# Feed-forward row pairs in one group of 12, masks summed early, last down products by output halves

## The chip, the cores and the metric

The kernel runs on one core of a Trainium2 chip. The metric is the device time of one execution in microseconds (us). Engines are named as in the profile: PE (TensorE) multiplies, PEld is its weight load, DVE is VectorE, ACT is ScalarE, POOL is GpSimd, SP only issues transfers here. PE writes its products to PSUM, eight banks of 512 float32 numbers per partition, and DVE and ACT read them from there.

## The reference

A row of 2048 tokens of 448 numbers goes through four layers: attention A, feed-forward B, A, B, with the same weights in both rounds.

```python
x = x + _A_ref(_layernorm(x), mem0, Wq, Wk, Wv, Wo, 32)
x = x + _B_ref(_layernorm(x), W_gate, W_up, W_down)
x = x + _A_ref(...)   # again, and B again
```

A runs over 64 segments of 32 tokens. Each segment is put behind a memory of 8 rows; 16 heads attend over these 40 rows (memory rows see all, token rows only earlier tokens); the first 8 rows of the output are the memory of the next segment. So the segments are a recurrence. B is, per token, `(relu(x Wg) * (x Wu)) Wd` with 1792 hidden numbers.

## The kernel before

Before the loop the kernel folds the weights: Wq with Wk into `A_sb`, Wv with Wo into `B_sb`, so that a step of the recurrence is: project the 40 rows by `A_sb` (PSUM tiles `prj`), scores of memory rows (`Sm`) and of token rows (`Sx`), softmax, weighting (`y`, `ya`, `yb`), projection by `B_sb` (`ox`, `o3`). The heads are taken in two halves, `hf` 0 and 1.

Both rounds run at once: chain 0 is the first A, chain 1 the second, four segments (LAG) behind. `step(g, ...)` (L679) does segment g of chain 0 and g-4 of chain 1. With two chains (g = 4 to 63) a step's matmuls have 80 columns, with one chain 40. Every second step, odd g from 3, also has a feed-forward: a `Feed` (L466) of 64 tokens of the first B and 64 of the second, 128 columns. The last two feeds have only 64. Steps run to g = 68; a tail behind them (L991 to L1008) finishes the last two feeds.

The order of work is written out by hand. `mm` (L142) chains all matmuls in the order in which the code issues them, and `InOrder` (L92) does so for DVE and ACT. So each engine is a queue in the order of the source, and an instruction that waits holds up all behind it on its engine. PSUM banks are given out by `bank` (L120): it takes the bank that, by a running estimate of PE's time (`now`) and a time `after` for each kind of tile, comes free first; `hold=True` keeps it until `let_go` (L130). A matmul into a bank waits for the last reader of the tile that was there.

A feed has 14 tiles of 128 hidden numbers, in groups u = 0 to 3 of 4, 4, 4 and 2. 448 input rows are three chunks of 128 and one of 64. The 64-row rest of Wu stands in partitions 0 to 63 of chunk 3, that of Wg in 64 to 127 (`FR`), and `xT` holds the rest of the tokens in both. `open_rows` (L493) issues these rests as row pairs: two matmuls of 64 rows each, one for `ups`, one for `gps`, which run side by side. It takes held banks, two a group. `products(u)` (L510) adds the three full chunks, 12 matmuls each for ups and gps, and lets the banks go. `gated(u)` (L521) copies ups to `ut` on ACT and writes `hh = max(gps, 0) * ut` on DVE. `down_part` (L530) multiplies `hh` by `Wd_sb` into `dps`, and `down_out` (L548) adds the residual and sends rows out.

`softmax` (L641) returns three closures: `first` (with two chains the mask is added into the SBUF tile `se`; then maximum and subtraction), `exp` on ACT, `second` (sum, reciprocal, and the product into `PM` or `PX`). m1, x0 and x1 are those of Sm and Sx of a half. `flipped` (L668) transposes PM or PX on PE (tile `pps`) and copies the result (`PT`). `weigh_m` (L749) makes ya and yb from PT and `hk`. `project_out(hf, t0, t1)` (L796) issues three ox matmuls for each of the tiles t0 to t1 of 28. `feed_on` (L572) turns the rows for the step after next into `hT` (through `tps`).

The part of a step with a feed around the change is L920 to L947, behind both `scores`: rows of groups 0 and 1, softmax x0, groups 0 and 1, flip of PM1, rows of groups 2 and 3, flip of PX0, group 2, weigh_m, group 3, all of softmax x1, 8 tiles of project_out, down, the rest. The last step with a feed (`end`, g = 67) is L904 to L919.

With one chain, the mask is a matmul of `ident` by `maskS` into Sx. With m and x both asked for, `scores` (L709) does the key chunks 0, 1, 3 of Sm, the mask, those of Sx, and then chunk 2 of both.

In the last two feeds `down_part` puts even tiles of hh in output partitions 0 to 63 and odd ones in 64 to 127, as column pairs side by side; `down_out` then copies the upper half by ACT (`other`), and DVE adds both to `x`.

Of the kernel before, what the change touches and what calls it, by code (L numbers as in the profile page):

```python
# [8 lines left out]
BF = mybir.dt.bfloat16  # L9
F32 = mybir.dt.float32  # L10
# [34 lines left out]

KD = (0, 1, 3, 2)
FR = (slice(0, 64), slice(64, 128))


def upper(hf, t):  # L50
# [9 lines left out]
def build_kernel(ctx, tc, A_x, A_mem0, A_Wq, A_Wk, A_Wv, A_Wo, B_W_gate, B_W_up, B_W_down, out,  # L60
# [69 lines left out]
    def let_go(t):  # L130

        i, after = bank_of[t.name]
        held.discard(i)
        free_at[i] = now[0] + after
# [80 lines left out]
    def weights(dst, src):  # L215
        return [(dst[:, k, cols], src[128 * k:128 * k + 128, cols])
                for k in range(3) for cols in (slice(0, F // 2), slice(F // 2, F))] + [
                    (dst[FR[src is B_W_gate], 3, :], src[384:448])]

    pieces = weights(Wu_sb, B_W_up)  # L220

    def next_piece():
# [235 lines left out]
    nc.gpsimd.memset(hh[:], 0.0)  # L458

    Wg_sb = main.tile([P, 4, F], BF, name="Wg_sb")  # L460
    pieces += weights(Wg_sb, B_W_gate)
    Wd_sb = main.tile([P, FT, DM], BF, name="Wd_sb")
    for f in range(FT):
# [2 lines left out]
    class Feed:  # L466
# [10 lines left out]
        def residual(self):  # L477
            tp = bank([P, 4, 128], BF, "otp")
            for kd in range(4):
                tr(tp[:, kd, :], OT[:, kd, :], ident[:])  # L480
            dve.tensor_tensor(self.x[:], tp[:].rearrange("p k d -> p (k d)")[:, 0:DM], self.x[:], op=ALU.add)
            self.st = row_stats(self.x)

        def norm(self):
            self.xn = normed(self.st)
# [7 lines left out]
        def open_rows(self, us):  # L493

            n = self.n
            self.ps = getattr(self, "ps", {})
            for u in us:
                self.ps[u] = [bank([P, 4, 128], F32, name, after, hold=True) for name, after in (("ups", 1000), ("gps", 1600))]
            for u in us:
                for e in range(min(4, FT - 4 * u)):  # L500
                    f = 4 * u + e
                    for W_sb, ps, rows in zip((Wu_sb, Wg_sb), self.ps[u], FR):
                        mm(ps[:, e, n], W_sb[rows, 3, f * 128:(f + 1) * 128], xT[rows, 3, n],
                           start=(e == 0), stop=False, skip_group_check=True)
# [5 lines left out]
        def products(self, u):  # L510
            n = self.n
            k = min(4, FT - 4 * u)
            for W_sb, ps in zip((Wu_sb, Wg_sb), self.ps[u]):
                for e in range(k):
                    f = 4 * u + e
                    for kd in range(3):
                        mm(ps[:, e, n], W_sb[:, kd, f * 128:(f + 1) * 128], xT[:, kd, n],
                           start=False, stop=(kd == 2), skip_group_check=True)
                let_go(ps)

        def gated(self, u):  # L521
            n = self.n
# [7 lines left out]
        def down_part(self, f0, f1):  # L530
            if f0 == 0:
                self.dps = bank([P, 512], F32, "dps", hold=True)
            dps = self.dps
            for f in range(f0, f1):
                if self.first:
                    mm(dps[:, 0:DM], hh[:, f, :], Wd_sb[:, f, :], start=(f == 0), stop=(f == FT - 1))
                else:
                    r = slice(64 * (f % 2), 64 * (f % 2) + 64)
                    mm(dps[r, 0:DM], hh[:, f, 0:TB], Wd_sb[:, f, :], start=(f < 2), stop=(f >= FT - 2),
                       tile_position=(0, r.start), skip_group_check=True)  # L540
            if f1 == FT:
                let_go(dps)

# [4 lines left out]
        def down_out(self):  # L548
            i, dps = self.i, self.dps
            if self.first:  # L550
                dve.tensor_tensor(self.nx[TB:P, :], dps[TB:P, 0:DM], self.x[TB:P, :], op=ALU.add)
                self.st = row_stats(self.nx)
                nc.sync.dma_start(xa[(i + 2) % 3][0:TB, :], self.nx[TB:P, :])
            if self.second and not self.first:
                other = main.tile([P, DM], F32, tag="other", name="other")
                act.copy(other[0:TB, :], dps[TB:P, 0:DM])
                dve.tensor_tensor(self.x[0:TB, :], dps[0:TB, 0:DM], self.x[0:TB, :], op=ALU.add)
                dve.tensor_tensor(self.x[0:TB, :], other[0:TB, :], self.x[0:TB, :], op=ALU.add)
                nc.sync.dma_start(out_dram[block(i - LAG // BLK)], self.x[0:TB, :])
            elif self.second:  # L560
                dve.tensor_tensor(self.x[0:TB, :], dps[0:TB, 0:DM], self.x[0:TB, :], op=ALU.add)
                nc.sync.dma_start(out_dram[block(i - LAG // BLK)], self.x[0:TB, :])
            if self.first and i + 3 < nblk:
                nc.sync.dma_start(self.x[TB:P, :], x_dram[block(i + 3)])
# [76 lines left out]
    def softmax(Sp, n, dst, keep, tag, mask=None):  # L641

        mx = main.tile([P, n], F32, tag=f"mx{tag}", name="mx")
        se = main.tile([P, n, L], F32, tag=f"se{tag}", name="se")
        ssum = main.tile([P, n], F32, tag=f"ssum{tag}", name="ssum")
        rs = main.tile([P, n], F32, tag=f"rs{tag}", name="rs")

        def first():
            src = Sp
            if mask is not None:  # L650
                dve.tensor_tensor(se[:], Sp[:], mask, op=ALU.add)
                src = se
            dve.tensor_reduce(mx[:], src[:], axis=AX.X, op=ALU.max)
            dve.tensor_tensor(se[:], src[:], mx[:].unsqueeze(2).to_broadcast([P, n, L]), op=ALU.subtract)

        def exp():
            act.activation(se[:], se[:], AF.Exp, scale=SCALE)

        def second():
            dve.tensor_reduce(ssum[:], se[:], axis=AX.X, op=ALU.add)  # L660
            dve.reciprocal(rs[:], ssum[:])
            if keep is not None:
                dve.tensor_tensor(rs[:], rs[:], keep, op=ALU.mult)
            dve.tensor_tensor(dst[:, :, 0:L], se[:], rs[:].unsqueeze(2).to_broadcast([P, n, L]), op=ALU.mult)

        return first, exp, second

    def flipped(src, n, tag, eng=dve):  # L668
        pps = bank([P, n, 128], BF, "pps")
# [9 lines left out]
    def step(g, ff, pre, late):  # L679
# [29 lines left out]
        def scores(hf, m, x):  # L709
# [21 lines left out]
                if not both:  # L731
                    mm(Sx[:, :, :], ident[:], maskS[:], start=True, stop=False, skip_group_check=True)

            if m and x:
                mem(KD[:3])
                mask()
                own(KD[:3])
                mem(KD[3:])
                own(KD[3:])
            elif m:  # L740
                mem(KD)
            elif x:
                mask()
                own(KD)
            sm = softmax(Sm, 2, PM[hf], blk[:], f"m{hf}") if m else (lambda: None,) * 3
            sx = softmax(Sx, 4, PX[hf], None, f"x{hf}", maskS[:] if both else None) if x else None
            return sm, sx

# [122 lines left out]
        def memory_0():  # L871
            nonlocal m0
            m0, _ = scores(0, True, False)
            m0[0]()
            m0[1]()

        if late is not None:
# [20 lines left out]
        _, x0 = scores(0, False, True)  # L898
        weigh_m(0, hk, pm)
        m1, x1 = scores(1, True, True)  # L900
        m1[0]()
        m1[1]()
        x0[0]()
        if end:  # L904
            ff.open_rows((0, 1))
            x0[1]()
            x1[0]()
            x1[1]()
            x0[2]()
            ff.products(0)  # L910
            ff.products(1)
            px0 = flipped(PX[0], 2, "x0", act)
            x1[2]()
            ff.gated(0)
            ff.gated(1)
            weigh_x(0, hk, px0)
            px1 = flipped(PX[1], 2, "x1", act)
            weigh_x(1, hk, px1)
            return {}, None  # L919
        if ff is not None:  # L920
            ff.open_rows((0, 1))
            x0[1]()
            m1[2]()
            x0[2]()
            feed(0, 1)
            next_piece()
            pm = flipped(PM[1], 1, "m1", act) if ms else None
            ff.open_rows((2, 3))
            px0 = flipped(PX[0], 2, "x0", act)
            feed(2)  # L930
            weigh_m(1, hk, pm)
            feed(3)
            x1[0]()
            x1[1]()
            x1[2]()
            ox_open()
            project_out(0, 0, 8)
            next_piece()
            ff.down()
            ff.norm2()  # L940
            project_out(0, 8, NT)
            project_last()
            next_piece()
            project_out(1, 0, 12)
            px1 = flipped(PX[1], 2, "x1")
            ff.feed_on()
            project_out(1, 12, NT)  # L947
        else:
            next_piece()
            ox_open()  # L950
            x0[1]()
            m1[2]()
            late_flip = 23
# [1 line left out]
            pm = flipped(PM[1], 1, "m1") if ms else None  # L955
            project_out(0, late_flip, NT)
            weigh_m(1, hk, pm)
            x1[0]()
            x1[1]()
            x0[2]()  # L960
# [28 lines left out]
            pre, late = step(g, None, pre, late)  # L989

    ff = Feed(nblk + LAG // BLK - 1)  # L991
    fed.open_rows((2, 3))
    ff.residual()
    for u in (2, 3):
        fed.products(u)
# [5 lines left out]
    ff.xposed()  # L1001
    ff.xposed_out()
    fed.down_out()
    for us in ((0, 1), (2, 3)):
        ff.open_rows(us)
        for u in us:
            ff.gate_up(u)
    ff.down()  # L1008


# [56 lines left out]
```

## Time and profile before

| what | value |
| --- | --- |
| median of 3 runs | 1585.41 us (1585.05 to 1586.82) |
| the profiled execution | 1585.9 us |
| its span | 1583.8 us |
| PE busy | 1570.4 us (99%) |
| DVE busy | 1130.9 us (71%) |
| ACT busy | 753.1 us (48%) |
| POOL busy | 77.4 us (5%) |
| mean granted PE clock | 0.998 |

The span runs from the first to the last instruction of the trace. "Busy" of PE is modelled, since matmuls overlap; a matmul's cost in a stream is the distance of its start to the next start, not its duration. A timeline line gives start, duration, engine, line of the code, operation, tiles (written <- read), shapes, how many were merged into it, and in brackets how long the engine had been idle and what ended that. L101, L143 and L151 are the helpers through which most instructions are recorded, so tiles tell them apart. The chain of waits is followed back from the last instruction to what released each.

### The profile page before, as it was taken

Reading aid. Unit: us, or ns where it says so; the run is one execution under the profiler, and the core shown is the slowest. Engines: PE = TensorE matmul, PEld = TensorE weight load, DVE = VectorE, ACT = ScalarE, POOL = GpSimd, SP = SyncE. Lnnn points to the kernel's source line nnn. Section 1 sums busy time; section 2 is a strip of 40 time slices with the busy share of each in tenths; the row PEclk is TensorE's granted clock in tenths of the full one; section 3 lists DMA queues with packets and bytes.
Section 4 is the critical chain, followed back from the end, with each engine's and each line's share of the span. In section 5 each row is a group of like instructions: output and inputs, shape, how many; then the busy total and the mean of one; then the engine's idle time right before and its main releaser. Section 6 shows DMA issues by size and latency. Waiting matters only on the chain.

```text
span 1583.8 us, 89753 instructions
## 1 busy us (share of the span) xinstructions
PE 1570.4 (99%) x41132; PEld 1444.0 (91%) x41132; DVE 1130.9 (71%) x3706; ACT 753.1 (48%) x2090; POOL 77.4 (5%) x172
## 2 busy tenths in 40 slices
PE   9999999999999999999999999999999999999998
PEld 6698999999999999999999999999999999999897
DVE  8766777777677777776777777767777777677764
ACT  5754444454444444544444445444444454444443
POOL 3200000000000000000000000000000000000000
PEclk9999999999999999999999999999999999999999
DMA  8620000000000000000000000000000000000000
GB/s 245 202 78 9 8 10 9 8 5 10 9 10 9 10 10 9 4 10 10 9 10 9 9 9 4 10 10 9 10 9 10 9 4 10 9 8 6 7 7 6
DMA packets 27755, 33.12 MB, mean 21 GB/s; under 512 B 3560, under 2 KB 26480, under 8 KB 27376
## 3 DMA queue, kind: packets, MB, share of 16 engines
q1 hardware_dynamic: 26288, 23.70, 5.4%
q8 instruction: 321, 5.26, 1.4%
q0 software_dynamic: 1088, 3.68, 0.8%
q14 instruction: 58, 0.48, 0.1%
HBM read 23.70 MB, written 1.84 MB: 16 GB/s over the span
## 4 chain that ended last, share of the span: by engine, by line
PE 97%; DVE 1%; ACT 0%; DMA 0%; issue 0%; SPq 0%; POOLq 0%; POOL 0%; ACTq 0%
PE prj L143 31%; PE ox L143 25%; PE ups L143 7%; PE dps L143 5%; PE gps L143 5%; PE o L143 5%; PE y L143 4%; PE Sx L143 3%; PE pps L151 2%; PE bps L143 1%; PE aps L143 1%; PE Sm L143 1%; PE tpw L151 1%; PE ya L143 1%; PE kps L151 1%; PE tps L151 1%
## 5 line engine op out<-in xcount | busy, mean ns | idle before, releaser
L143 PE MATMUL prj<-hT,A_sb 128*128 128x80 bf16 (+3 forms) x15232 | 541.6, 199 | 0.1
L143 PEld LDWEIGHTS <-A_sb 128*128 128x128 bf16 (+1 forms) x15232 | 498.5, 99 | 23.0 <-issue 0.6
L143 PEld LDWEIGHTS <-B_sb 128*128 128x128 bf16 (+1 forms) x15232 | 492.7, 103 | 13.7 <-issue 0.2
L143 PE MATMUL ox<-Y,B_sb 128*128 128x80 bf16 (+3 forms) x11424 | 441.7, 200 | 0.1
L101 ACT CAST TQ<-prj 128x480 bf16<-128x480 f32 (+1 forms) x380 | 184.2, 497 | 102.9 <-PE prj L143 96.2
L101 ACT CAST Y<-y 128x512 bf16<-128x512 f32 (+2 forms) x392 | 137.2, 419 | 94.8 <-PE y L143 94.6
L101 DVE CAST Y<-y 128x256 bf16<-128x256 f32 x376 | 151.4, 457 | 42.2 <-PE y L143 42.0
L101 ACT ACTIVATE se<-se 128x80 f32<-128x80 f32 (+1 forms) x270 | 81.9, 303 | 181.3 <-DVE se L101 177.0
L143 PE MATMUL gps<-xT,Wg_sb 128*128 128x128 bf16 (+3 forms) x1904 | 137.2, 215 | 0.0
L143 PE MATMUL ups<-xT,Wu_sb 128*128 128x128 bf16 (+3 forms) x1904 | 134.7, 216 | 0.5 <-DVE xT L101 0.5
L101 DVE CAST TQ<-prj 128x480 bf16<-128x480 f32 (+1 forms) x228 | 128.6, 573 | 6.8 <-PE prj L143 6.4
L143 PEld LDWEIGHTS <-Wu_sb 128*128 128x128 bf16 (+1 forms) x1904 | 106.1, 97 | 10.3
L143 PEld LDWEIGHTS <-hk 40*128 40x128 bf16 (+1 forms) x1950 | 99.7, 96 | 14.1 <-issue 3.0
L101 DVE SCALAR_TENSOR_TENSOR hh<-gps,ut 128x512 bf16<-128x512 f32 (+2 forms) x136 | 77.6, 591 | 45.0 <-PE ya L143 40.7
L143 PEld LDWEIGHTS <-Wg_sb 128*128 128x128 bf16 (+1 forms) x1904 | 108.0, 97 | 0.5 <-issue 0.5
L101 ACT CAST TZ<-prj 64x320 bf16<-64x320 f32 (+2 forms) x264 | 96.9, 378 | 17.2 <-DVE TZ L101 13.6
L101 ACT COPY os<-o 64x16 f32<-64x16 f32 (+3 forms) x135 | 25.7, 191 | 163.2 <-PE o L143 161.6
L101 DVE TENSOR_REDUCE ssum<-se 128x2 f32<-128x80 f32 (+1 forms) x270 | 73.8, 273 | 37.1 <-ACT se L101 37.1
L143 PE MATMUL y<-PT,hk 40*128 40x256 bf16 (+1 forms) x1280 | 91.2, 248 | 1.9 <-ACT PT L101 1.0
L143 PE MATMUL dps<-Wd_sb,hh 128*128 128x448 bf16 (+1 forms) x476 | 93.1, 353 | 0.0
L143 PEld LDWEIGHTS <-TQ 128*128 128x128 bf16 x1938 | 86.7, 97 | 1.6 <-issue 1.3
L101 ACT COPY PT<-pps 128x256 bf16<-128x256 bf16 (+1 forms) x136 | 47.2, 347 | 81.1 <-PE pps L151 76.9
(118 smaller groups left out, 1881.1 us busy)
## 6 DMA issues: line engine op xcount, KB each, us to landing
wo<-in_A_Wo_dram POOLq DMA_DIRECT2D x8, 448.0 KB, 5.1
nat<-in_A_Wq_dram SPq DMA_DIRECT2D x8, 384.0 KB, 5.0
nat<-in_A_Wk_dram SPq DMA_DIRECT2D x8, 384.0 KB, 4.8
nat<-in_A_Wv_dram SPq DMA_DIRECT2D x8, 384.0 KB, 4.3
xa<-in_A_x_dram SPq DMA_DIRECT2D x32, 56.0 KB, 2.2
xa<-xp SPq DMA_DIRECT2D x32, 56.0 KB, 1.9
out_dram<-xa SPq DMA_DIRECT2D x32, 56.0 KB, 2.1
xp<-in_A_x_dram SPq DMA_DIRECT2D x30, 56.0 KB, 2.5
```

The source lines that it names most:

```text
L101: r = f(*a, **k)
L143: in_order(nc.tensor.matmul(out, lhsT, rhs, **k))
L151: in_order(nc.tensor.transpose(out, src, idn))
```

## The change

- `products(3)`, the last two tiles, no longer has row pairs: it takes one new bank for both ups and gps and issues four full chunks each (16 matmuls), the halves of the other weight in chunk 3 being set to zero by two memsets on POOL.
- In steps with a feed the three other groups' row pairs are one group of 12, behind the first 10 tiles of project_out. The softmax of x1 (`x1[0]`, `x1[1]`) now stands ahead of group 0, its last part between the products of group 1 and their gating. Eight more tiles of project_out stand ahead of down, 10 behind it; of half 1, 18 stand ahead of feed_on.
- `softmax` returns a fourth closure, `lift`: with two chains the mask sum alone, with one chain maximum and subtraction; `first` does what is left. m1 and both Sx are lifted before anything else.
- With one chain, `scores` does all of Sm, then the mask, then Sx.
- The last step with a feed puts group 1 between the flips of PX0 and PX1.
- The last two feeds' down product uses two column halves of 224 outputs for each tile of hh, side by side in partitions 0 to 63 and 64 to 127; the residual is brought into the same layout (`xh`) by two transfers, one DVE addition follows, and two transfers go out.
- The tail opens the rows of one group for one feed, and of three for the other.

```diff
+    nc.gpsimd.memset(Wu_sb[64:128, 3, 12 * 128:F], 0.0)
...
+    nc.gpsimd.memset(Wg_sb[0:64, 3, 12 * 128:F], 0.0)
...
+            if not self.first:
+                self.xh = main.tile([P, DM // 2], BF, tag="xh", name="xh", bufs=2)
+                for c in range(2):
+                    nc.sync.dma_start(self.xh[64 * c:64 * c + 64, :], self.x[0:TB, HALF[c]])
...
-            for W_sb, ps in zip((Wu_sb, Wg_sb), self.ps[u]):
+            if u == 3:
+                both = bank([P, 2, 2, 128], F32, "gps", 1600)
+                self.ps[3] = [both[:, 0], both[:, 1]]
+            for which, (W_sb, ps) in enumerate(zip((Wu_sb, Wg_sb), self.ps[u])):
                 for e in range(k):
                     f = 4 * u + e
-                    for kd in range(3):
+                    for kd in range(3 if u < 3 else 4):
...
-                    r = slice(64 * (f % 2), 64 * (f % 2) + 64)
-                    mm(dps[r, 0:DM], hh[:, f, 0:TB], Wd_sb[:, f, :], start=(f < 2), stop=(f >= FT - 2),
-                       tile_position=(0, r.start), skip_group_check=True)
+                    for c in range(2):
+                        mm(dps[64 * c:64 * c + 64, 0:DM // 2], hh[:, f, 0:TB], Wd_sb[:, f, HALF[c]],
+                           start=(f == 0), stop=(f == FT - 1), tile_position=(0, 64 * c), skip_group_check=True)
...
-                other = main.tile([P, DM], F32, tag="other", name="other")
-                act.copy(other[0:TB, :], dps[TB:P, 0:DM])
-                dve.tensor_tensor(self.x[0:TB, :], dps[0:TB, 0:DM], self.x[0:TB, :], op=ALU.add)
-                dve.tensor_tensor(self.x[0:TB, :], other[0:TB, :], self.x[0:TB, :], op=ALU.add)
-                nc.sync.dma_start(out_dram[block(i - LAG // BLK)], self.x[0:TB, :])
+                dve.tensor_tensor(self.xh[:], dps[:, 0:DM // 2], self.xh[:], op=ALU.add)
+                for c in range(2):
+                    nc.sync.dma_start(out_dram[block(i - LAG // BLK), HALF[c]], self.xh[64 * c:64 * c + 64, :])
...
-        def first():
-            src = Sp
+        def lift():
             if mask is not None:
                 dve.tensor_tensor(se[:], Sp[:], mask, op=ALU.add)
-                src = se
+            else:
+                shift(Sp)
+
+        def first():
+            if mask is not None:
+                shift(se)
+
+        def shift(src):
             dve.tensor_reduce(mx[:], src[:], axis=AX.X, op=ALU.max)
             dve.tensor_tensor(se[:], src[:], mx[:].unsqueeze(2).to_broadcast([P, n, L]), op=ALU.subtract)
...
-            if m and x:
+            if m and x and not both:
+                mem(KD)
+                mask()
+                own(KD)
+            elif m and x:
                 mem(KD[:3])
-                mask()
...
-        m1[0]()
+        m1[3]()
         m1[1]()
-        x0[0]()
+        x0[3]()
         if end:
+            x1[3]()
             ff.open_rows((0, 1))
             x0[1]()
-            x1[0]()
             x1[1]()
             x0[2]()
             ff.products(0)
+            px0 = flipped(PX[0], 2, "x0", act)
+            ff.gated(0)
             ff.products(1)
-            px0 = flipped(PX[0], 2, "x0", act)
             x1[2]()
-            ff.gated(0)
+            px1 = flipped(PX[1], 2, "x1", act)
             ff.gated(1)
             weigh_x(0, hk, px0)
-            px1 = flipped(PX[1], 2, "x1", act)
             weigh_x(1, hk, px1)
             return {}, None
         if ff is not None:
-            ff.open_rows((0, 1))
+            x1[3]()
+            ox_open()
+            project_out(0, 0, 10)
+            ff.open_rows((0, 1, 2))
+            x0[0]()
             x0[1]()
             m1[2]()
             x0[2]()
-            feed(0, 1)
-            next_piece()
-            pm = flipped(PM[1], 1, "m1", act) if ms else None
-            ff.open_rows((2, 3))
-            px0 = flipped(PX[0], 2, "x0", act)
-            feed(2)
-            weigh_m(1, hk, pm)
-            feed(3)
             x1[0]()
             x1[1]()
+            feed(0)
+            next_piece()
+            ff.products(1)
             x1[2]()
-            ox_open()
-            project_out(0, 0, 8)
+            pm = flipped(PM[1], 1, "m1", act) if ms else None
+            ff.gated(1)
+            ff.products(2)
+            px0 = flipped(PX[0], 2, "x0", act)
+            weigh_m(1, hk, pm)
+            ff.gated(2)
+            feed(3)
+            project_out(0, 10, 18)
             next_piece()
             ff.down()
             ff.norm2()
-            project_out(0, 8, NT)
+            project_out(0, 18, NT)
             project_last()
             next_piece()
             project_out(1, 0, 12)
             px1 = flipped(PX[1], 2, "x1")
+            project_out(1, 12, 18)
             ff.feed_on()
-            project_out(1, 12, NT)
+            project_out(1, 18, NT)
...
-    fed.open_rows((2, 3))
+    fed.open_rows((2,))
...
-    for us in ((0, 1), (2, 3)):
-        ff.open_rows(us)
-        for u in us:
-            ff.gate_up(u)
+    ff.open_rows((0, 1, 2))
+    for u in range(4):
+        ff.gate_up(u)
```

## The prediction

> **What bounds the kernel now.** First the page: the span, the busy times and the engines of the chain that ended last.
>
> ```profile
> span 1583.8 us, 89753 instructions
> PE 1570.4 (99%) x41132; PEld 1444.0 (91%) x41132; DVE 1130.9 (71%) x3706; ACT 753.1 (48%) x2090; POOL 77.4 (5%) x172
> PE 97%; DVE 1%; ACT 0%; DMA 0%; issue 0%; SPq 0%; POOLq 0%; POOL 0%; ACTq 0%
> ```
>
> PE sets the time. The chain in order of time repeats itself: its dps entries come at 761.34 and 806.59, and so on, 45.25 us for two steps, one of them with a feed-forward ("feed"). So one period tells about thirty. I read the feed step that begins near 799 in the timelines, engine by engine. PE first (start, duration, instruction, count):
>
> ```profile
> 802.50 0.22 PE L151 MATMUL pps<-ident,PM 128*128 128x128 bf16 x1
> 802.65 0.23 PE L143 MATMUL ups<-xT,Wu_sb 64*128 64x128 bf16 x1
> ...
> 802.89 0.22 PE L143 MATMUL ups<-xT,Wu_sb 64*128 64x128 bf16 x1
> 803.00 0.21 PE L143 MATMUL gps<-xT,Wg_sb 64*128 64x128 bf16 x1
> 803.01 0.23 PE L143 MATMUL ups<-xT,Wu_sb 64*128 64x128 bf16 x1
> 803.06 0.21 PE L143 MATMUL gps<-xT,Wg_sb 64*128 64x128 bf16 x1
> 803.21 0.29 PE L151 MATMUL pps<-ident,PX 128*128 128x128 bf16 x2
> 803.33 0.83 PE L143 MATMUL ups<-xT,Wu_sb 128*128 128x128 bf16 x12
> 804.00 0.83 PE L143 MATMUL gps<-xT,Wg_sb 128*128 128x128 bf16 x12
> ```
>
> Durations overlap, so starts count: 12 full products take 0.67 (0.056 each), and so does each row pair inside the group. Going from a full matmul to a row pair takes 0.15 in place of 0.056, and back again 0.15. Between 802.89 and 803.00 the pair's second half waits: its bank is freed by the gating hh of group 0, which starts at 802.27 on VectorE and takes 0.68. So a freed bank is used 0.05 after the reader's end.
>
> Now VectorE in the same step, and ScalarE:
>
> ```profile
> 799.27 0.24 DVE L101 TENSOR_REDUCE mx<-Sm 128x2 f32<-128x80 f32 x1
> 799.54 0.24 DVE L101 TENSOR_TENSOR se<-Sm,mx 128x80 f32<-128x80 f32 x1
> 799.70 0.31 DVE L101 TENSOR_TENSOR se<-Sx,maskS 128x160 f32<-128x160 f32 x1
> 800.05 0.32 DVE L101 TENSOR_REDUCE mx<-se 128x4 f32<-128x160 f32 x1
> 800.40 0.33 DVE L101 TENSOR_TENSOR se<-se,mx 128x160 f32<-128x160 f32 x1
> 800.64 0.23 DVE L101 TENSOR_REDUCE ssum<-se 128x2 f32<-128x80 f32 x1
> ...
> 802.27 1.28 DVE L101 SCALAR_TENSOR_TENSOR hh<-gps,ut 128x512 bf16<-128x512 f32 x2
> ```
>
> ```profile
> 800.82 0.34 ACT L101 ACTIVATE se<-se 128x160 f32<-128x160 f32 x1 [0.68 <-DVE se L101]
> 801.07 0.57 ACT L101 CAST ut<-ups 128x512 bf16<-128x512 f32 x1
> ```
>
> An operation that needs the one before starts 0.35 after it (160 elements); one that doesn't, 0.24. An exponential starts 0.09 after its subtraction ends, and the copy ut stands behind it on ScalarE. Between 802.27 and 806.2 VectorE handles only gatings and a copy; the softmax of x1 comes behind them.
>
> **The change, part by part.**
>
> *Row pairs in one group (all feeds).* Gone: the second group. From 802.50 to 803.21 are 0.71, less the flip's own 0.06: 0.65. Added: its four remaining pairs in the first group, 4 x 0.056 = 0.22, and four more full products in the last two tiles (16 for 12), 0.22. Entry after ox (not in this place before; ox to row pairs of prj at 815.89 costs 0.01 more than after Sx) and the first ox waiting for the copy of ya (ends 799.14; 0.02): +0.03. PE's own work falls by 0.65-0.22-0.22-0.03 = 0.18 per feed. Ahead of down stand 54 ox matmuls in place of 24 (10 and 8 tiles of three for 8); these 30 are only moved: 30 x 0.036 = 1.08.
>
> *What VectorE and ScalarE now do first.* In the changed order both mask sums come first, then x0's and x1's reduction and subtraction and x1's exponential, all ahead of ut and the gating of group 0; then x1's sum, reciprocal and PX; only then the gating of group 1. And by the changed program's bank assignment (the same wait in all 30 feeds of two chains) the new bank of the last two tiles is that of gps group 1: PE may start them only after the gating of group 1. Step by step, from 799.27, which doesn't move:
> - subtraction m 799.54, mask sum x0 799.70, mask sum x1 799.94 (+0.24), reduction x0 800.18, subtraction 800.53, m's sum to PM 0.24+0.26+0.20+0.20 -> 801.43, x0's sum 801.59, reciprocal 801.94, PX 802.15, reduction x1 802.39, subtraction x1 802.75, ending 803.08.
> - ScalarE: exponential x1 at 803.17; ut of group 0 at 803.42 (+0.25, as above), ending 803.99.
> - gating of group 0 at 804.07, x1's sum 804.67 (+0.60: the two gatings of 1.28, one of which takes 0.68), reciprocal 805.02, PX 805.23, gating of group 1 at 805.47, ending 806.16. PE may go on at 806.21.
>
> PE on its side: ox from 799.20, 30 x 0.036; row pairs 800.38 to 801.15; groups 0 and 1, 48 x 0.056, to 803.83; the flip of PM1, whose bank is freed by ut of group 0, at 804.04 (wait of 0.21); group 2 to 805.44; flip of PX0 and ya, yb to 805.79. There it stands until 806.21: **a wait of 0.42**. What queues behind it on PE is everything: 16 products (0.89), 24 ox (0.86), down at 807.96. Before, down starts at 806.42; 807.96-806.42-1.08 = **+0.46 per feed** in place of -0.18. The flip's wait doesn't add, since VectorE's chain ends the second wait anyway. Gatings 2 and 3 end by about 807.95; down reaches their rows 1.5 and 2.3 after its start. Behind down, SP's transfers follow the same additions as before. feed_on comes 18 ox later than before, so fewer stand behind it: hT's copy on ScalarE ends 1.12 after the first tps (813.85 to 814.97), PE has 0.22 of tps, 30 ox of 1.08 and a switch of 0.10 until the row pairs need it: 0.2 to spare.
>
> 30 feeds (g = 5 to 63) have two chains: +13.8. In the two with one chain (g = 3, 65) there is no mask sum, the exponential of x1 comes early, PE decides: 2 x -0.18 = -0.4.
>
> *Last step with a feed (g = 67).* Before: the flips of PX0 and PX1 are followed by 0.73 each of waiting for their copies. Now group 1 lies between. But PX0 is only there at 1558.72 (PE waits about 0.6), ut and gating 0 come ahead of x1's sum, so PX1 ends at 1561.06, and its flip, copy and y follow: ox starts near 1562.5 for 1561.58: +0.9. After these waits the clock falls even now (window, then PE busy ... , granted clock, DMA share, GB/s):
>
> ```profile
> 1558.40:1561.80 3.40, 2.37 (x44) 1.84 (x41) 2.34 (x8) 2.09 (x6) 0.00 (x0) 1.00 0.00 0
> 1561.80:1565.20 3.40, 3.40 (x70) 3.40 (x67) 0.00 (x0) 0.69 (x3) 0.00 (x0) 0.50 0.02 5
> ```
>
> A window at 0.50 costs 1.7; it may vanish, stay or double: 0, +-1.7 in the range.
>
> *The end.* One group and one switch less: -0.16. Last product: 14 pairs of 224 columns for 7 of 448, the same streaming; twice the weight loads, between free (the 56 matmuls of o, each with a 64-column load, take 1.12 from 811.32: 0.02 each) and 14 x 0.11 = 1.6, the mean of such a load by itself; free taken, by the row of o, which is nearest. Now ACT's copy (1578.78, 0.53) and two additions (1579.34, 1579.99, 0.62 each) lead to the DMA at 1580.63. One addition of 128x224 isn't in the trace: between 0.3 (128x160) and 0.62 (64x448), 0.36 taken, nearest to the copy of 128x256 at 0.42. It starts at about 1578.7, the DMA at 1579.1, the second half one issue (0.47) later: -1.1. The xh transfers (two per feed, some 2 us like xa<-xp) go out at 1570.7 and are needed at 1578.7: hidden. Together -1.3.
>
> *The rest.* Mask order in one-chain steps: TQ's copy ends at 1542.31, Sm's last needs it at 1542.38: 0 to 0.05 in seven steps, 0. Two memsets on POOL, idle 95%: 0 to 0.5, 0.
>
> **Sum:** 13.8-0.4+0.9-1.3 = +13.0 on a span of 1583.8 (execution 1585.9, 2.1 around the span, so 1598.9). The median of the runs lies 0.5 lower, at 1585.4: **1598.4 us**.
>
> **Rivals.**
> - *PE decides (faster).* If VectorE's chain ended 0.64 earlier (or the banks were free), each feed wins 0.18: 30 x -0.18 - 0.8 = -6: 1579. The point from which it decides: the chain from 799.27 to 806.16 must be shorter than 6.43, not 6.9, for a gain at all, and 6.25 for all of it. For it: the spacings come from other surroundings. Against it: each step is a measured spacing, and the order of issue is fixed. 8%.
> - *No change:* PE waits only for the flip's 0.21, which uses up the 0.18: 30 x 0.03 - 0.8: 1585.5. 4%.
> - *The delay goes on:* gating or hT's copy (0.2 ahead) becomes late too, +0.4 more per feed: 1610. 6%.
> - *The clock falls in each feed:* the waits of 0.21 and 0.42 lie in one window of 3.4; a window at half clock costs 1.7, 30 of them 51: 1650. The window before the slow one holds about 1.5 of 3.4 of streaming (its few matmuls times their spacings); the new one keeps 2.7. 2%. The Trainium skill, "TensorE: Matmul & The Clock Gate", section "A second HAM failure mode: psum-queue depth-cycling", says that cycling through PSUM banks leaves PE idle often enough to make the clock swing. No feed in this trace shows that.
>
> **Numbers.** Forecast 80%. Its bounds: 0.1 off in the chain is 3.0 over 30 feeds; with 1.7 for a clock window and 1.6 for loads, about 1592 to 1605. A run tells 0.2% (3.2 us) from no change: slower 0.88, same 0.04, faster 0.08.
>
> **What would show it.** Period near 45.7 in the chain; in each feed step an idle stretch on PE just before the last two tiles' products, ended by hh of group 1; ut of group 0 directly behind x1's exponential; gating 0 starting near 4.8 after the reduction of Sm (3.0 now); one row group a feed; the last DMA issue less than 1.1 after the last product's end. Wrong if PE shows no gap there, or if the period is 45.06.

## The result and the profile after

The changed kernel takes **1600.88 us** (median of 5 runs, 1599.81 to 1601.73); the kernel before takes 1585.41 (5 runs, 1584.3 to 1586.82). The ratio is 1.0096, with a 95% interval of 1.0081 to 1.011. The prediction was 1598.4, in a range of 1592 to 1605.

The page of the changed kernel, its span, busy times and the engines of the chain that ended last. The helpers' lines have moved by one: L102, L144 and L152 are L101, L143 and L151 of before.

```profile
span 1599.0 us, 89723 instructions
...
PE 1574.0 (98%) x41160; PEld 1450.5 (91%) x41160; DVE 1124.8 (70%) x3704; ACT 744.1 (47%) x2088; POOL 78.2 (5%) x174
...
PE 90%; DVE 7%; issue 1%; ACT 1%; SPq 0%; DMA 0%; POOL 0%; POOLq 0%; ACTq 0%
```

Busy time doesn't explain it: VectorE and ScalarE are even a little less busy, and PE's modelled busy time grew by 3.6 us (28 more matmuls), a quarter of what the span grew by. What has changed is the chain: VectorE, 1% of it before, now holds 7%. Work that lay beside TensorE's now lies on the path.

How long one period is, read from the first matmul of down in two neighbouring feeds (the timeline, TensorE alone):

```profile
770.70 1.11 PE L144 MATMUL dps<-Wd_sb,hh 128*128 128x448 bf16 x5
...
816.32 0.92 PE L144 MATMUL dps<-Wd_sb,hh 128*128 128x448 bf16 x4
```

That is 45.62 us, against 45.24 before (first matmul to first matmul, the usual distance in the trace); the chain of waits before has the same two entries 45.25 apart (start, length, what):

```profile
761.34 2.65 PE dps L143 x14
...
806.59 2.65 PE dps L143 x14
```

So 0.38 more in each of 29 periods. The chain of waits after the change, between its two lines above, in order of time:

```profile
811.09 0.67 PE ups L144 x12
811.76 0.68 PE gps L144 x12
812.44 0.68 DVE hh L102
813.12 0.24 DVE ssum L102
813.35 0.02 issue
813.38 0.19 DVE rs L102
813.57 0.02 issue
813.59 0.04 DVE PX L102
813.62 0.21 issue
813.83 0.69 DVE hh L102
814.53 0.04 issue
814.57 1.05 PE gps L144 x16
815.62 0.86 PE ox L144 x24
```

Here the path leaves TensorE, goes through the gating of group 0, x1's sum, reciprocal and product and the gating of group 1, and comes back to TensorE at the last two tiles (16 matmuls). Why the first gating is as late as 812.43, the timeline of the same step tells:

```profile
811.16 0.33 DVE L102 TENSOR_TENSOR se<-se,mx 128x160 f32<-128x160 f32 x1
...
811.58 0.34 ACT L102 ACTIVATE se<-se 128x160 f32<-128x160 f32 x1 [1.88 <-DVE se L102]
...
811.83 0.57 ACT L102 CAST ut<-ups 128x512 bf16<-128x512 f32 x1
...
812.43 0.69 DVE L102 SCALAR_TENSOR_TENSOR hh<-gps,ut 128x512 bf16<-128x512 f32 x1 [0.94 <-PE gps L144]
812.45 0.22 PE L152 MATMUL pps<-ident,PM 128*128 128x128 bf16 x1
...
814.57 0.61 PE L144 MATMUL gps<-xT,Wu_sb 128*128 128x128 bf16 x8 [0.23 <-DVE hh L102]
```

ScalarE stands idle for 1.88 until x1's subtraction is done, because the exponential is first in its queue; ut of group 0, whose product had long been there, comes behind it, and VectorE, idle for 0.94, waits for ut, which ends at 812.40, 0.03 before the gating starts. The bracket, and the chain above, name the gps products of group 1 instead, whose modelled end comes 0.02 later; but this gating reads group 0. An inferred releaser has to be held against the code. By start-to-start distances the two waits on TensorE are 0.18 at the flip of PM1 and 0.40 ahead of the last two tiles. The list of TensorE's waits has the second one in 29 feeds; before it had no such entry:

```profile
PE gps L144 <- DVE hh L102: 6.7, 29, 0.2
```

Its 0.23 each is the idle time behind the modelled end of the matmul before; the 0.40 is what the stream loses.

Where the 15.3 us of span came from (1599.03 less 1583.76), by the delay against before at a landmark that each step has (the transposition of the rows to `hk`, at the end that of o):

| stretch | predicted | measured |
| --- | --- | --- |
| steps g = 0 to 2, no feed | 0 | +1.4 |
| g = 3 and 65, one chain, feed | -0.4 | +0.7, +0.1 |
| g = 5, two chains, feed of 64 columns | +0.46 | +1.5 |
| 29 feeds of 128 columns | +13.3 | +11.2 |
| g = 67, last step with a feed | +0.9 | +1.0 |
| tail | -1.3 | -0.5 |

### The profile page after: what moved, and what is told of

Same layout as the page of the kernel before. It is cut to its first block, busy times and chain, and to the rows that moved or that the text cites. A ratio compares the mean times of both kernels' runs of the same rounds, so it can differ in the third digit from the quotient of the medians.

```text
span 1599.0 us, 89723 instructions
## 1 busy us (share of the span) xinstructions
PE 1574.0 (98%) x41160; PEld 1450.5 (91%) x41160; DVE 1124.8 (70%) x3704; ACT 744.1 (47%) x2088; POOL 78.2 (5%) x174
## 4 chain that ended last, share of the span: by engine, by line
PE 90%; DVE 7%; issue 1%; ACT 1%; SPq 0%; DMA 0%; POOL 0%; POOLq 0%; ACTq 0%
PE prj L144 31%; PE ox L144 24%; PE dps L144 5%; PE o L144 5%; PE y L144 4%; PE gps L144 4%; PE Sx L144 3%; PE ups L144 3%; DVE hh L102 3%; PE bps L144 1%; DVE se L102 1%; PE aps L144 1%; PE Sm L144 1%; PE pps L152 1%; PE tpw L152 1%
## 5 line engine op out<-in xcount | busy, mean ns | idle before, releaser
L144 PE MATMUL prj<-hT,A_sb 128*128 128x80 bf16 (+3 forms) x15232 | 541.7, 199 | 0.7 <-issue 0.5
L144 PEld LDWEIGHTS <-A_sb 128*128 128x128 bf16 (+1 forms) x15232 | 498.7, 99 | 23.5 <-issue 1.1
L144 PEld LDWEIGHTS <-B_sb 128*128 128x128 bf16 (+1 forms) x15232 | 497.5, 103 | 14.3 <-issue 0.6
L144 PE MATMUL ox<-Y,B_sb 128*128 128x80 bf16 (+3 forms) x11424 | 450.4, 200 | 0.6 <-issue 0.5
L102 ACT CAST TQ<-prj 128x480 bf16<-128x480 f32 (+1 forms) x380 | 184.5, 497 | 103.2 <-PE prj L144 96.5
L102 DVE CAST Y<-y 128x256 bf16<-128x256 f32 x376 | 151.3, 457 | 42.5 <-PE y L144 42.4
L102 ACT CAST Y<-y 128x512 bf16<-128x512 f32 (+2 forms) x392 | 137.1, 419 | 73.7 <-PE y L144 73.6
L102 ACT ACTIVATE se<-se 128x80 f32<-128x80 f32 (+1 forms) x270 | 81.9, 303 | 192.1 <-DVE se L102 187.8
L102 DVE CAST TQ<-prj 128x480 bf16<-128x480 f32 (+1 forms) x228 | 128.6, 573 | 6.8 <-PE prj L144 6.3
L144 PE MATMUL gps<-xT,Wg_sb 128*128 128x128 bf16 (+3 forms) x1904 | 128.5, 215 | 0.0
L144 PEld LDWEIGHTS <-Wu_sb 128*128 128x128 bf16 (+1 forms) x1904 | 106.8, 97 | 22.3 <-issue 13.0
L102 DVE SCALAR_TENSOR_TENSOR hh<-gps,ut 128x512 bf16<-128x512 f32 (+2 forms) x136 | 80.8, 595 | 50.7 <-ACT ut L102 33.3
L144 PEld LDWEIGHTS <-hk 40*128 40x128 bf16 (+1 forms) x1950 | 99.6, 96 | 13.5 <-issue 2.3
L102 ACT COPY os<-o 64x16 f32<-64x16 f32 (+3 forms) x135 | 25.8, 191 | 176.4 <-PE o L144 174.8
L144 PE MATMUL ups<-xT,Wu_sb 128*128 128x128 bf16 (+3 forms) x1632 | 106.7, 216 | 0.5 <-DVE xT L102 0.5
L144 PEld LDWEIGHTS <-Wg_sb 128*128 128x128 bf16 (+1 forms) x1904 | 106.7, 97 | 0.5 <-issue 0.5
L102 ACT CAST TZ<-prj 64x320 bf16<-64x320 f32 (+2 forms) x264 | 97.0, 378 | 17.2 <-DVE TZ L102 13.6
L144 PE MATMUL dps<-Wd_sb,hh 128*128 128x448 bf16 (+1 forms) x504 | 93.1, 342 | 0.0
L102 ACT COPY PT<-pps 128x256 bf16<-128x256 bf16 (+1 forms) x136 | 47.3, 347 | 97.4 <-PE pps L152 97.4
L144 PE MATMUL y<-PT,hk 40*128 40x256 bf16 (+1 forms) x1280 | 91.2, 248 | 0.9 <-ACT Y L102 0.8
L102 DVE TENSOR_REDUCE ssum<-se 128x2 f32<-128x80 f32 (+1 forms) x270 | 73.3, 272 | 24.2 <-ACT se L102 24.2
L144 PEld LDWEIGHTS <-TQ 128*128 128x128 bf16 x1938 | 86.7, 97 | 1.7 <-issue 1.3
```

What stands on the lines that cost most here:

```text
L102: r = f(*a, **k)
L144: in_order(nc.tensor.matmul(out, lhsT, rhs, **k))
```

## Experiments

Each variant was timed beside the kernel before on the same chip, and ratios are against that one. "Distance" is that from one dps to the next.

**1. x1's softmax behind the gatings again.**

```diff
-            x1[0]()
-            x1[1]()
             feed(0)
             next_piece()
             ff.products(1)
-            x1[2]()
...
             feed(3)
+            x1[0]()
+            x1[1]()
+            x1[2]()
             project_out(0, 10, 18)
```

> Changed kernel, but x1's maximum, subtraction, exponential, sum and product to PX1 stand behind the gating of group 3 again, as before the change; the mask sums, the one group of 12 row pairs and the full products of the last two tiles stay. Theory (x1's exponential ahead of ut of group 0 on ScalarE, and x1's sum ahead of the gating of group 1 on VectorE, make TensorE wait 0.18 at the flip of PM1 and 0.40 ahead of the last two tiles): both waits go, the distance of one dps to the next falls from 45.62 to 45.04 us, the time to about 1582. Rival (the single group itself costs TensorE: changes between row pairs and full products, 16 full products for 12): the distance stays above 45.4, the time above 1593.

Measured: distance 45.10, 1584.23 us, ratio 0.9992 (0.9982 to 1.0001). Both waits are gone and with them 0.52 per feed; the single group doesn't cost, it saves 0.14. The rival is out. The distance misses the expected 45.04 by 0.06: ut of group 1 now stands on ScalarE behind the copy PT of PM1, so that the gating of group 1 ends (849.60) just ahead of the products that take its bank (849.66), with nothing to spare. Experiment 5, where the bank is another one, has 45.05.

**2. One instruction moved: the exponential behind ut.**

```diff
             x1[0]()
-            x1[1]()
             feed(0)
+            x1[1]()
             next_piece()
```

> Changed kernel, with one instruction moved: x1's exponential on ScalarE stands behind ut of group 0 in place of ahead of it. All of VectorE's work keeps its order. Theory (the link of the chain is ScalarE's queue, ut behind an exponential that waits for x1's subtraction): ut of group 0 starts about 2 us earlier, the gating of group 0 directly behind x1's subtraction, the gating of group 1 ends about 0.9 earlier, before TensorE needs its bank; both waits go: 45.04, about 1582. Rival (VectorE's own work for x1, some 1.5 us ahead of the gating of group 1, is what TensorE waits for): the wait ahead of the last two tiles stays at 0.2 or more, distance 45.25 or more, time above 1588.

Measured: distance 45.105, 1584.74 us, ratio 0.9996 (0.9986 to 1.0005). VectorE does the same work in the same order, and yet both waits go. Its step in the timeline:

```profile
848.30 0.32 DVE L102 TENSOR_TENSOR se<-se,mx 128x160 f32<-128x160 f32 x1
...
848.54 0.68 DVE L102 SCALAR_TENSOR_TENSOR hh<-gps,ut 128x512 bf16<-128x512 f32 x1
...
848.72 0.34 ACT L102 ACTIVATE se<-se 128x160 f32<-128x160 f32 x1 [0.53 <-DVE se L102]
...
850.45 0.69 DVE L102 SCALAR_TENSOR_TENSOR hh<-gps,ut 128x512 bf16<-128x512 f32 x1 [0.43 <-ACT ut L102]
...
851.20 0.61 PE L144 MATMUL gps<-xT,Wu_sb 128*128 128x128 bf16 x8
```

Start to start, the gating of group 0 comes 0.24 after x1's subtraction, where it was 1.27 in the changed kernel (811.16 to 812.43). The gating of group 1 ends 0.51 earlier (6.29 behind the reduction of Sm in place of 6.80), not 0.9: it now waits for ut of group 1, which stands behind the copy PT on ScalarE. So the link of the chain that decides is ScalarE's queue, not VectorE's amount of work.

**3. Another bank for the last two tiles** (`pick`, a new parameter of `bank`, names it).

```diff
-                both = bank([P, 2, 2, 128], F32, "gps", 1600)
+                both = bank([P, 2, 2, 128], F32, "gps", 1600, pick=sx_bank[0])
...
+            if x and hf == 1:
+                sx_bank[0] = bank_of[Sx.name][0]
```

> Changed kernel, all orders kept; the last two tiles of the feed-forward get the bank that Sx of half 1 has left (its only reader is the early mask sum) in place of the bank that the gating of group 1 frees. Theory (the 0.40 is a wait for a bank, not for data): it goes and nothing takes its place, since down needs the gatings of groups 2 and 3 only 1.5 and 2.3 us after its start; the wait of 0.18 at the flip of PM1 stays: distance 45.22, time about 1588. Rival (TensorE is held up by VectorE's chain anyway, next at down or at the flip of PX0): distance stays near 45.6, time near 1600.

Measured: distance 45.22, 1587.37 us, ratio 1.0008 (0.9998 to 1.0017). The wait of 0.40 was one for a bank; VectorE's chain is as long as in the changed kernel (6.80 to the end of the second gating), and TensorE doesn't wait for its end, as the timeline of one step shows:

```profile
806.03 0.68 DVE L102 SCALAR_TENSOR_TENSOR hh<-gps,ut 128x512 bf16<-128x512 f32 x1
...
806.37 0.61 PE L145 MATMUL gps<-xT,Wu_sb 128*128 128x128 bf16 x8
```

What stays above experiment 5's 45.05 is 0.17, the flip's wait.

**4. A dose: one more addition ahead of the gating of group 1.**

```diff
+            dve.tensor_tensor(extra[:], extra[:], maskS[:], op=ALU.add)
             ff.gated(1)
             ff.products(2)
```

> Changed kernel, and one more addition of 128x160 on VectorE, of numbers that nobody reads, between PX1 and the gating of group 1 in each of the 32 steps with a feed. Theory (VectorE's chain up to that gating sets each period): the addition's spacing of 0.24 comes back in full, distance 45.86, time about 1608. Rival (something else sets the period, and VectorE is idle 30% of the time): no change, 45.62, 1601.

Measured: distance 45.85, 1608.25 us, ratio 1.0141 (1.0126 to 1.0156). The addition's spacing comes back whole (+0.235), though VectorE is busy for 71% of the span. The list of waits doubles its entry:

```profile
PE gps L144 <- DVE hh L102: 13.6, 29, 0.5
```

This run answers a second question. Its first steps (g = 0 to 2) are the same code as in the changed kernel, and they end 0.2 later than before the change, not 1.4 (see the table above).

**5. Both cures.** The changes of experiments 2 and 3 together.

> Changed kernel with both cures together: x1's exponential behind ut of group 0, and the last two tiles in the bank that Sx of half 1 has left. Theory: TensorE waits nowhere in a feed of 128 columns and only its own work is left, distance 45.10 as in each run in which both waits were gone; the first feed of 64 columns (g = 3) loses the 0.7 that it lost with the old bank: about 1583. Rival (some further limit lies right behind): distance stays above 45.2.

Measured: distance 45.05, 1580.84 us, ratio 0.997 (0.9959 to 0.9981). TensorE waits for nothing in the feeds of 128 columns, and its own work is 0.19 less than before. The 2.2 us that g = 3 and 5 had lost are gone too (their delay is -0.1 each).

**6. Both cures, and the last step with a feed in its old order.**

```diff
-            x1[3]()
             ff.open_rows((0, 1))
             x0[1]()
+            x1[3]()
...
             ff.products(0)
-            px0 = flipped(PX[0], 2, "x0", act)
-            ff.gated(0)
             ff.products(1)
+            px0 = flipped(PX[0], 2, "x0", act)
             x1[2]()
-            px1 = flipped(PX[1], 2, "x1", act)
+            ff.gated(0)
             ff.gated(1)
             weigh_x(0, hk, px0)
+            px1 = flipped(PX[1], 2, "x1", act)
             weigh_x(1, hk, px1)
```

> As the kernel with both cures, but the last step with a feed (g = 67) in its old order, flips of PX0 and PX1 behind groups 0 and 1. Theory (the new order puts ut and gating of group 0 ahead of x1's sum, and so PX1 and all behind it about 1 us later): from the first transposition of the residual in g = 65 to that of o in the step behind, 20.3 us, or 21.7 with a window of half clock in it, where the changed kernel has 22.8 with such a window and three variants of it 21.2 to 21.4 without; time about 1582. Rival (the order of this step is worth nothing, and only the window differs): the same 21.3 without a window.

Measured: 1578.97 us, ratio 0.9959 (0.9945 to 0.9972), 0.4% less than the kernel before. The stretch that is compared runs from the transposition of the residual in g = 67 to that of the normalized rows in the tail (the expectation's numbers are of this stretch, though it names other steps). It took 21.65 with a window at half clock, against 22.77 with one in the changed kernel: the new order costs 1.1. The flip of PX1 starts 8.97 behind the first of these transpositions, as before the change, where the changed kernel has 9.82: 0.85 of the 1.1 is there already. Experiment 5, with the new order, had no such window and took 21.3; the old order without one wasn't seen.

**7. Both cures, the last down product in its old form,** with its copy on ScalarE, two additions and one transfer.

```diff
-                    for c in range(2):
-                        mm(dps[64 * c:64 * c + 64, 0:DM // 2], hh[:, f, 0:TB], Wd_sb[:, f, HALF[c]],
...
+                    r = slice(64 * (f % 2), 64 * (f % 2) + 64)
+                    mm(dps[r, 0:DM], hh[:, f, 0:TB], Wd_sb[:, f, :], start=(f < 2), stop=(f >= FT - 2),
```

> As the kernel with both cures, but the last feeds' down product in its old form: even and odd tiles side by side, copy on ScalarE, two additions of 64x448, one transfer. Theory (the halves save the copy and one addition, and cost one transfer's issue): from the start of the last down product to the end of the span 6.6 us, as before the change, where the changed kernel has 6.15. Rival (the gain of 0.4 comes from the order of the last feeds' groups): 6.15 here too.

Measured, in one profiled execution: 6.98 from the last dps to the end of the span, 6.20 in experiment 5. So the halves gain 0.8 from there on, and the order of the groups nothing; the rival is out. What the order gains lies ahead of the last dps: 7.24 from the transposition of o to it, 7.39 before the change. That 6.98 isn't the 6.6 of before shows in what SP waits for at the close of each program, first before the change, then in this variant:

```profile
SPq L1062 <- PEq L1062: 0.7, 2, 0.5
```

```profile
SPq L1090 <- PEq L1090: 1.1, 2, 0.9
```

The changed kernel has 1.1 there too. What lengthens this closing wait for TensorE's sequencer wasn't tried.

**8. The suspect alone, in the kernel before.**

```diff
             x0[2]()
-            feed(0, 1)
+            x1[0]()
+            x1[1]()
+            feed(0)
+            ff.products(1)
+            x1[2]()
+            ff.gated(1)
...
             feed(3)
-            x1[0]()
-            x1[1]()
-            x1[2]()
```

> Kernel before the change, with one part of the change alone: in steps with a feed x1's mask sum, maximum, subtraction and exponential stand ahead of ut and gating of group 0, its sum and PX1 between the gatings of groups 0 and 1. Row pairs stay in two groups. Theory (x1 ahead of the gating is what costs, and in the old kernel TensorE waits for the gating of group 0 already at the second group of row pairs): that gating starts 1.96 later, and all of it shows: distance 47.2 in place of 45.24, time about 1645. Rival (it costs only together with the single group and the new bank): distance below 45.5, time below 1595.

Measured: 1667.45 us, ratio 1.0519 (1.0505 to 1.0533). x1's place alone does the harm: the gating of group 0 starts 4.96 after the reduction of Sm, as reckoned (3.00 and 1.96), and 19 of 29 distances are 47.2 to 47.5. The other ten are 48.8 to 48.9, and that is most of why the time is 22 us above the expectation. The second group's row pairs in the timeline:

```profile
270.66 0.21 PE L143 MATMUL ups<-xT,Wu_sb 64*128 64x128 bf16 x1 [1.20 <-ACT ut L101]
...
271.39 0.21 PE L143 MATMUL gps<-xT,Wg_sb 64*128 64x128 bf16 x1 [0.51 <-DVE hh L101]
```

and four windows of 3.41 us, each pair a window with these waits and the one behind it (window, length, busy of PE, PEld, DVE, ACT and POOL, granted clock, DMA share, GB/s):

```profile
268.45:271.86 3.41, 1.70 (x30) 1.25 (x28) 2.34 (x8) 1.46 (x4) 0.00 (x0) 1.00 0.00 0
271.86:275.28 3.42, 3.42 (x37) 3.42 (x35) 1.72 (x4) 1.28 (x3) 0.00 (x0) 0.50 0.02 5
1033.03:1036.44 3.41, 1.76 (x31) 1.41 (x29) 2.34 (x9) 1.46 (x4) 0.00 (x0) 1.00 0.02 5
1036.44:1039.85 3.41, 3.35 (x69) 3.25 (x69) 2.69 (x8) 1.65 (x4) 0.00 (x0) 1.00 0.00 0
```

The stretches at half clock are 3.413 us long, and their starts lie whole multiples of that apart (271.86 and the last one of a feed, 1514.31: 364 times). Against this fixed grid the same waits lie at two places. In the first pair they lie within one window, 1.70 of it is busy, and the next window runs at half clock, which costs 1.6; in the second pair the end of the waits falls into the next window, 1.76 is busy, and the clock stays.

## Why the prediction was right, and where it was off

**The mechanism** was right, step by step: the order of issue puts x1's exponential ahead of ut of group 0 on ScalarE and x1's last part ahead of the gating of group 1 on VectorE, and the new bank makes TensorE wait for that gating. Experiment 2 shows the first link, experiment 3 the bank, experiment 4 that the chain sets the period, experiment 8 that x1's place suffices without the rest of the change.

**The chain's length** from the reduction of Sm to the end of the second gating was put at 6.89 and is 6.80 (807.71 to 814.51); the gating of group 0 starts 4.72 behind it (4.80). Most of the 0.09 is one spacing that no row had given: the gating of group 0 was put 0.08 behind the end of ut and starts 0.03 behind it. Another 0.03 lies in spacings that I rounded up, ahead of the exponential (3.87 behind the reduction of Sm in place of 3.90). That accounts for 0.46 per feed having become 0.38, and for 2.2 us over 29 feeds.

**TensorE's own saving** of 0.18 per feed: 0.19 in experiment 5, where nothing else is left. The flip's wait (0.21) is 0.18.

**"In the two with one chain (g = 3, 65) ... PE decides"** is the step that failed. I reckoned by the number of chains and overlooked that the first two feeds have only 64 columns, for which TensorE's full products start 0.03 apart in place of 0.056, while the chain on ScalarE and VectorE keeps most of its length (6.05 at g = 5, 5.66 at g = 3, for 6.80). At g = 5 the changed kernel's timeline has

```profile
174.11 0.22 PE L152 MATMUL pps<-ident,PM 128*128 128x128 bf16 x1 [1.40 <-ACT ut L102]
...
176.24 0.39 PE L144 MATMUL gps<-xT,Wu_sb 128*128 128x64 bf16 x8 [0.79 <-ACT ut L102]
```

where the kernel before had

```profile
169.88 0.23 PE L151 MATMUL pps<-ident,PM 128*128 128x128 bf16 x1 [0.43 <-DVE PM L101]
...
170.68 0.28 PE L151 MATMUL pps<-ident,PX 128*128 128x128 bf16 x2 [0.29 <-DVE PX L101]
```

The difference, 2.19 less 0.72, is the 1.5 of the table. So g = 3, 5 and 65 cost 2.3 where the sum had 0.1. The second wait at g = 5 also shows that the new bank isn't that of the gating of group 1 "in all 30 feeds of two chains": here it is the one that ut of group 2 frees. Experiment 5 takes these losses away with both cures. At g = 3 the bank alone is the cause: the loss is still there in experiment 2 (0.7) and gone in experiment 3. At g = 5 each cure alone leaves a part (0.8 in experiment 2, 0.6 in experiment 3). TensorE still waits there in experiment 5, about as long as before the change:

```profile
172.31 0.27 PE L153 MATMUL pps<-ident,PX 128*128 128x128 bf16 x2 [0.81 <-ACT ut L102]
```

**The rest, "0":** the first three steps were 1.4 later in this execution. Nothing shows that they are the change's: experiments 1 to 7 share these steps with the changed kernel and end them 0.3 earlier to 1.2 later than before, experiments 5 to 7, the same code up to g = 67, differ by 1.5 among themselves, and experiment 8, which has the code of before in these steps, ends them 1.1 later than the kernel before did. TensorE stops there for 0.2 to 0.85 at changing places, and the profile names nothing that it waits for ("issue"), while the weights of the feed-forward come in by DMA. What holds it up stays open.

**The last step, +0.9:** 1.1 like for like (experiment 6), and PX1's late sum was the reason given; its flip is 0.85 late. **The end, -1.3:** -0.5. The group and the switch less give the 0.15 that was reckoned (-0.16). The addition does end 1.43 earlier behind the last dps (1.96 in place of 3.39), about as reckoned. But the span ends 4.2 behind it in place of 3.2, where I had put 0.47 for the second transfer. Experiment 7, with one transfer, ends 3.6 behind its last addition: so 0.4 of this 1.0 comes without the second transfer, as much as the closing wait grew by, and 0.6 with it.

**The rivals.** "PE decides" needs the chain below 6.43 for a gain and below 6.25 for all of it, or the banks free. Experiments 1 and 2 have a chain of 6.29 and gain 0.14 per feed, experiment 5 has the bank free and gains 0.19: the sizes were right, the changed kernel's chain just isn't that short. "No change", a wait for the flip alone, is what experiment 3 leaves (45.22). "The delay goes on" didn't come: with the dose of experiment 4 there is still nothing late behind the gating but the 0.24 itself. "The clock falls in each feed" didn't come in the changed kernel, nor with the dose (waits of 0.18 and 0.63); it did in experiment 8 in ten feeds of 29. This bears out the direction of what the Trainium skill says ("TensorE: Matmul & The Clock Gate", section "A second HAM failure mode: psum-queue depth-cycling"): cycling through PSUM banks can leave TensorE idle often enough for its clock to swing. In these feeds it took 1.7 us of idle time in a window of 3.41; in the last step with a feed, before the change, 1.0 was enough (2.37 of 3.40 busy, the prediction's row).

The sum came within 2.5 us, but partly by luck, since terms cancel: the 29 feeds 2.2 too high, the feeds of 64 columns and one chain 2.2 too low, the start 1.4 and the tail 0.8 too low.

## What to carry to other kernels

An engine that is busy for 70% can still set the period: what counts is the queue order on each engine between a product and the reader that frees its bank. Before an operation is moved ahead, follow all its parts on every engine; one early exponential on ScalarE, which is idle for half of the time, held up a copy, a gating, a bank and so TensorE. Then look at the steps in which the bounding engine has less to do (here the feeds of 64 columns), since a chain of fixed length shows there first, and most.

## What the runs showed of the hardware

- The granted clock goes by a fixed grid of 3.413 us (worked out at experiment 8), and there a few hundredths of a microsecond decide: windows with 1.70 us busy were followed by half clock, one with 1.76 was not. So a longer wait can cost in jumps of 1.6.
- Busy time by the profile isn't the rule. In the last step with a feed a window of the grid with 1.95 busy came ahead of one at half clock in the changed kernel, and one with 1.72 busy did not in experiment 4. The code is the same there, and the stretch compared in experiment 6 takes 1.4 us less in experiment 4 (21.36 in place of 22.77). The two windows:

```profile
1574.17:1577.58 3.41, 1.95 (x31) 1.40 (x27) 1.86 (x7) 1.72 (x6) 0.00 (x0) 1.00 0.00 0
...
1578.62:1582.03 3.41, 1.72 (x50) 1.48 (x47) 2.16 (x8) 1.13 (x4) 0.00 (x0) 1.00 0.02 5
```

- Going from full products to row pairs and back costs as reckoned (0.13 and 0.15 in place of 0.04 and 0.06), so that the one group of 12 saves one such pair of changes per feed.
- A bank is taken up 0.05 to 0.06 after the end of its reader (gating ends 814.51, product starts 814.57); in experiments 1 and 2 too.
